# Moving the channel moves and the result stores of a chunked recurrence kernel from SyncE's queue to GpSimd's

## The chip, the cores and the metric

The kernel runs on one core of one Trainium2 chip. The metric is the device time of one execution, in microseconds. Five engines take part: TensorE (PE, with its weight loads shown apart as PEld), VectorE (DVE), ScalarE (ACT), GpSimd (POOL) and SyncE (SP). Each works through its own instructions in order, and semaphores tie them together. A transfer (DMA) is issued by an engine as one of its instructions and then runs by itself.

## The reference

Two parts follow each other: a recurrence over 768 steps for 4 × 8 heads with a 40 × 40 state each, and on its output (4 × 768 × 320) a gated layer with a short convolution in time.

```python
for t in range(S):                      # S = 768; B, H, D = 4, 8, 40
    y[:, :, t] = einsum('bhd,bhde->bhe', r_t, state)
    Sa = einsum('bhde,bhe->bhd', state, a_t)
    state = state * w_t[:, :, None, :] - einsum('bhd,bhe->bhde', Sa, b_t)
    state = state + einsum('bhd,bhe->bhde', v_t, k_t)
x = y.transpose(0, 2, 1, 3).reshape(B, S, H * D)
gate_pre = sum(conv_w[k] * xp[:, k:k + S] for k in range(5))   # xp: x with 4 zero rows ahead
out = (sigmoid(gate_pre) * (x @ w_val)) @ w_out
```

## The kernel before

The 768 steps are cut into 24 chunks of 32. Inside a chunk the recurrence becomes matrix products and a small triangular solve; the state goes from chunk to chunk. All of this stands in `fast_path`. A second path (`general_path`) runs only when a decay lies outside a range; with these inputs it does not run.

Per chunk c, in the names of the plan: `load` brings `ew` (decays, k, b and a; three buffers), `load2` brings `va` and `w` (v in two layouts), `load3` brings `rv` (r, v and r again; one buffer). `rs`, `vs`, `rs1` and `es` (lines 458, 462 and 465) are ScalarE's copies out of `rv`; the next `load3` waits for them. `am`, `u0`, `ut`, `u`, `g`, `ysa`, `ysb` are TensorE's products; `evac_s` makes the next state, `evac_y` (line 532) writes the chunk's output into the tile `xe`, whose rows are heads and positions within a head.

Two chunks make a group for the gated layer; the last two chunks are groups of one, so there are 13 groups. For a group, `xd` moves the outputs from `xe` into the tile `xt`, whose rows are channels: twelve transfers from on-chip memory to on-chip memory, in two halves of eight and four (`x_moves`, line 71). Then come the convolution `cv` (ScalarE line 656, VectorE line 658), the gate (lines 668 to 673), the products `val` (lines 89, 97) and `gv` (line 688), `out` (lines 107, 114), ScalarE's copy `os` (line 703), and `store`, two transfers of 160 KB into the result. Group number gi uses half gi % 2 of the tile `XTW`; its copies `os` go into that same half, which `val` has read by then. So the moves of group gi wait, beside other things, until the stores of group gi − 2 have landed: the list `xw` on line 645 has `("store", pg, 0)` and `("store", pg, 1)`.

What sets the order is `Plan.order`: each step is entered with an engine, an estimated duration in ns and the steps it waits for; a list scheduler runs over these estimates and gives each engine its sequence. TensorE, ScalarE, VectorE and GpSimd carry out exactly that sequence (line 713). SyncE's transfers are not in that list of engines; the framework orders them. In the plan SyncE is nevertheless one engine with durations, so what it is thought to be busy with moves the steps of the others too. Where TensorE would be idle the plan also puts filler products on a constant tile (line 726). The products `val` and `out` of a group are held back until certain later products of the recurrence (`when`, line 679).

Before the change SyncE issues all transfers, and the only line that does it is 317, in the helper `dma`. GpSimd clears three tiles at the start (lines 336, 337, 624) and has nothing to do after that.

Of the kernel before, what the change touches and what calls it, by code (L numbers as in the profile page):

```python
# [16 lines left out]
B, H, S, D = 4, 8, 768, 40  # L17
C = 32
P16 = 16
ER = 104  # L20
DM = 320
# [22 lines left out]
def ac(n):  # L44
    return 154 + 0.833 * n
# [25 lines left out]
def x_moves(xt, xe, L, hf):  # L71

    for h, e0, e1, k, r in (X0, X1)[hf]:
        src = xe[h % 2 * 64 + e0:h % 2 * 64 + e1, h // 2 * 4:h // 2 * 4 + 4, 0:L + 4]
        if k < 2:
            yield xt[r:r + e1 - e0, 4 * k:4 * k + 4, 0:L + 4], src
        else:
            for j in range(2):
                yield xt[j * 64 + r:j * 64 + r + e1 - e0, 8:10, 0:L + 4], src[:, 2 * j:2 * j + 2]
# [20 lines left out]
def out_mms(nc, ps, gv, wo, j, n):  # L100
    T = nc.tensor
    L = n * C
    if n == 2:
        for k in range(3):
            r = slice(j * 64, j * 64 + 64) if k == 2 else slice(0, 128)
            q = 8 if k == 2 else 4 * k + 2 * j
            T.matmul(out=ps, lhsT=gv[r, q * L:q * L + 128], rhs=wo[k][r], start=(k == 0), stop=(k == 2))  # L107
    else:
        for k in range(3):
            for h in range(2):  # L110
                r = slice(h * 64, h * 64 + 64)
                rk = r if k == 2 else slice(0, 128)
                q = 8 * L if k == 2 else (4 * k + 2 * h) * L
                T.matmul(out=ps[r], lhsT=gv[rk, q:q + 64], rhs=wo[k][rk], start=(k == 0), stop=(k == 2))
# [37 lines left out]
class Plan:  # L152
# [6 lines left out]
    def op(self, name, eng, dur, deps, fn, lat=None, give=None):  # L159
        assert name not in self.ops, name  # L160
        self.ops[name] = [eng, dur, list(deps), fn, LAT if lat is None else lat]
        if give:
            self.gives[name] = list(give)
# [100 lines left out]
def fast_path(ctx, tc, ins, out, nch, cst, wts, wz, wmx):  # L264
# [3 lines left out]
    V, A, G, T = nc.vector, nc.scalar, nc.gpsimd, nc.tensor  # L268
# [15 lines left out]
    XTW = const.tile([128, 2 * 680], F32, name="xt")  # L284
# [15 lines left out]
    op = plan.op  # L300

    sg, groups = [], []
    c = 0
    while c < nch:
        n = min(nch - c, 4 if sg else 2)
        sg.append((c, n))
        c += n
    c = 0
    while c < nch:
        n = 2 if c + 2 < nch else 1  # L310
# [5 lines left out]
    def dma(o, i):  # L316
        nc.sync.dma_start(out=o, in_=i)  # L317

    def B2(nm, c):
        return (nm, c, 0), (nm, c, 1)  # L320
# [213 lines left out]
    def slot(nm):  # L534
        return st_["slot", nm]
# [99 lines left out]
    for gi, (c, n) in enumerate(groups):  # L635
        L = n * C
# [4 lines left out]

        def xd(hf, c=c, xt=xt, L=L):
            for o, i in x_moves(xt, st_["xe", c], L, hf):
                dma(o, i)
        xw = [x for j in range(n) for x in B2("evac_y", c + j)] + wl + [("cv", pg, 4, 0), ("cv", pg, 4, 1), ("cv", pg, 4, 2), ("val", pg, 2), ("store", pg, 0), ("store", pg, 1)]
        for hf in range(2):
            op(("xd", c, hf), "SP", (5200, 2600)[hf], xw, lambda hf=hf, xd=xd: xd(hf), 2200)
        xds = [("xd", c, 0), ("xd", c, 1)]
        op(("xd", c), "SP", 1, xds, lambda: None, 2200)
        acc, gv = [AG[:, i * 640:i * 640 + 10 * L].rearrange("p (b t) -> p b t", t=L) for i in range(2)]  # L650
# [43 lines left out]
        for j in range(n):  # L694
            def outm(j=j, c=c, n=n, gf=gf):
                out_mms(nc, slot(("out", c, j))[:, 0:DM], gf, wo, j, n)
            nm = ("out", c, j)
            op(nm, "PE", 1980, prev_gv + om + ([] if late else [when[3 + j]]), outm, give=[("os", c, j)])
            om = [nm]
            prev_out.append(nm)  # L700

            def osc(j=j, c=c, xo=gi % 2 * 680):
                A.copy(out=XTW[:, xo + j * DM:xo + (j + 1) * DM], in_=slot(("out", c, j))[:, 0:DM])
            op(("os", c, j), "ACT", ac(DM), om, osc)

            def store(j=j, c=c, n=n, L=L, xo=gi % 2 * 680):
                dma(out[j * B // n:(j + 1) * B // n, c * C:c * C + L], XTW[:, xo + j * DM:xo + (j + 1) * DM])
            op(("store", c, j), "SP", 800, [("os", c, j)], store, 2200)

    A.preload_act_table_set("natural_log_exp_and_others")  # L710
    E_ = mybir.EngineType
# [1 line left out]
    with tc.manual_schedule(engines={E_.PE, E_.Activation, E_.DVE, E_.Pool}):  # L713
# [3 lines left out]
        for t, e, d, n, fn, s in seq:  # L717
            if s is not None:
                st_["slot", n] = PF[s]
            if e == "PE":  # L720
                lev = min(lev, CAP) - RHO * (t - at)
                at = t
                i = min(range(NS), key=lambda i: free[i])
# [74 lines left out]
def rwkv_kernel(tc, ins, out, nch):  # L798
    with ExitStack() as outer:
        keep = outer.enter_context(tc.tile_pool(name="keep", bufs=1))  # L800
        cst = keep.tile([128, NCST], F32, name="cst")
        wts = keep.tile([128, NWT], F32, name="wts")
        wz = keep.tile([128, 2, DM], F32, name="wz")
        wmx = keep.tile([ER, nch, 2], F32, name="wmx")
        with ExitStack() as ctx:
            fast_path(ctx, tc, ins, out, nch, cst, wts, wz, wmx)
        general_path(tc, ins, out, nch, cst, wts, wz, wmx)
# [69 lines left out]
```

## Time and profile before

| | |
|---|---|
| time, median of 3 runs | 592.12 us (586.3 to 593.3) |
| time of the profiled execution | 591.55 us |
| its span, first to last instruction | 589.5 us |
| busy: PE, DVE, ACT, POOL | 436.1, 408.4, 325.4, 2.5 us |
| mean granted TensorE clock | 0.845 |
| transferred | 58.82 MB, mean 100 GB/s |
| moves `xt<-xe`, stores `out<-xt` | 156 and 24, all issued by SyncE |

The span has three parts: until about 90 us first loads and preparation for several chunks; until about 550 us the chunks one after the other, about 19 us each, with the gated layer of earlier groups between them; then the gated layer of the last groups alone. A row of a group reads: line, engine, operation, output and input tile, count, busy time, mean of one, idle time of the engine just before and what ended it. A row of the waits reads: who waited for whom, total us, times, longest. "SPq" is SyncE issuing a transfer or waiting to.

### The profile page before, as it was taken

The numbers are of one execution on the slowest core, as the hardware profiler recorded it, in microseconds if no ns is written. First come the engines' busy times: TensorE is split into PE (matmuls) and PEld (weight loads), VectorE is DVE, ScalarE is ACT, GpSimd is POOL, SyncE is SP. The second block draws the span as 40 slices with busy tenths as digits, with TensorE's granted clock in tenths as the row PEclk, the third lists the DMA queues.
The fourth block names the chain that finished last, engine by engine and source line by source line (L and its number), as shares of the span: only waits on it lengthen the run. The fifth ranks groups of instructions, "written<-read, shape, count | busy, mean of one in ns | idle before, by whom it ended". The sixth has DMA issues, their size and how long they took to land.

```text
span 589.5 us, 21830 instructions
## 1 busy us (share of the span) xinstructions
PE 436.1 (74%) x9599; PEld 370.1 (63%) x9599; DVE 408.4 (69%) x1025; ACT 325.4 (55%) x652; POOL 2.5 (0%) x8
## 2 busy tenths in 40 slices
PE   4625148983887878889597785879976799789752
PEld 4624137873876767668576675758855677668541
DVE  5379897698887597797485767768965687643230
ACT  4549615554576675787547575764836363554220
POOL 1000000000000000000000000000000000000000
PEclk8857659696999788997797888888997899899866
DMA  8857740242457346445423843514151433311100
GB/s 189 215 135 166 174 121 27 72 97 63 87 131 178 95 112 147 89 126 129 111 53 75 192 101 78 135 53 97 35 138 54 97 92 95 97 43 22 33 19 16
DMA packets 23924, 58.82 MB, mean 100 GB/s; under 512 B 6057, under 2 KB 16553, under 8 KB 21329
## 3 DMA queue, kind: packets, MB, share of 16 engines
q1 hardware_dynamic: 23825, 57.38, 40.3%
q8 instruction: 77, 1.26, 0.9%
q14 instruction: 22, 0.18, 0.1%
HBM read 49.23 MB, written 3.93 MB: 90 GB/s over the span
## 4 chain that ended last, share of the span: by engine, by line
PE 40%; DMA 20%; DVE 17%; ACT 12%; issue 6%; SPq 5%; DVEq 0%; ACTq 0%
DMA rv<-in_rv 6%; PE pc L487 6%; SPq L317 5%; PE pc L508 5%; PE pf L89 4%; DMA ew<-in_ew 4%; DMA out<-xt 4%; PE pf L499 3%; PE pf L411 3%; PE pf L107 3%; DMA w<-in_vw 3%; PE pf L385 3%; PE pc L483 3%; DVE ag L658 3%; PE pc L470 2%
## 5 line engine op out<-in xcount | busy, mean ns | idle before, releaser
L658 DVE SCALAR_TENSOR_TENSOR ag<-xt,wts,ag 128x256 f32<-128x256 f32 (+1 forms) x156 | 60.7, 418 | 32.2 <-ACT ag L656 32.2
L426 DVE TENSOR_TENSOR tm<-x 128x30 f32<-128x30 f32 (+14 forms) x210 | 68.5, 326 | 1.2
L429 DVE TENSOR_TENSOR x<-x,tm 128x30 f32<-128x30 f32 (+14 forms) x210 | 68.4, 326 | 1.1
L458 ACT ACTIVATE rb<-rv,cst 104x512 f32<-104x512 f32 x48 | 34.5, 718 | 48.2 <-DMA rv<-in_rv 48.1
L385 PE MATMUL pf<-kb,qb 104*64 104x64 f32 x768 | 34.6, 258 | 32.6 <-DVE x L429 13.9
L385 PEld LDWEIGHTS pf<-kb,qb 104*64 104x64 f32 x768 | 31.4, 169 | 35.6 <-ACT er L351 18.5
L487 PE MATMUL pc<-ub,T 64*32 64x80 f32 x768 | 39.7, 260 | 12.5 <-issue 9.9
L411 PE MATMUL pf<-cst,kb 104*128 104x104 f32 x192 | 28.6, 290 | 27.3 <-DVE ak L400 18.3
L107 PE MATMUL pf<-wts,ag 128*128 128x320 f32 x132 | 47.5, 483 | 0.0
L726 PE MATMUL pf<-dm 128*128 128x128 f32 x246 | 45.5, 347 | 2.7 <-DVE dm L714 1.1
L351 ACT ACTIVATE er<-ew,bias 104x512 f32<-104x512 f32 x48 | 34.5, 719 | 20.6 <-DVE y L368 12.7
L726 PEld LDWEIGHTS pf<-dm 128*128 128x128 f32 x246 | 40.4, 251 | 5.9 <-issue 2.0
L483 PE MATMUL pc<-T,ub 64*40 64x32 f32 x1536 | 23.4, 215 | 26.9 <-DVE T L441 14.3
L487 PEld LDWEIGHTS pc<-ub,T 64*32 64x32 f32 x768 | 33.2, 123 | 15.9 <-issue 11.7
L89 PE MATMUL pf<-xt,wts 128*128 128x128 f32 (+1 forms) x208 | 37.7, 307 | 7.2 <-DMA xt<-xe 7.2
L346 DVE TENSOR_TENSOR_SCAN lam<-ew,ind 104x528 f32<-104x528 f32 x24 | 30.1, 1255 | 16.4 <-DMA ew<-in_ew 16.4
L499 PE MATMUL pf<-rb,vu 104*64 104x64 f32 x768 | 33.2, 251 | 10.6 <-ACT vu L491 8.0
L502 DVE TENSOR_TENSOR w<-pf,cst 128x512 f32<-128x512 f32 x24 | 16.6, 692 | 34.9 <-PE pf L499 28.0
L411 PEld LDWEIGHTS pf<-cst,kb 104*128 104x128 f32 x192 | 21.1, 158 | 31.1 <-DVE ak L400 18.5
L483 PEld LDWEIGHTS pc<-T,ub 64*40 64x40 f32 x1536 | 20.3, 134 | 32.0 <-ACT ub L478 12.1
L508 PE MATMUL pc<-w,kbt 64*40 64x72 f32 x1536 | 34.1, 236 | 7.8 <-issue 4.4
L499 PEld LDWEIGHTS pf<-rb,vu 104*64 104x64 f32 x768 | 29.5, 162 | 16.2 <-ACT vu L491 11.7
(91 smaller groups left out, 885.2 us busy)
## 6 DMA issues: line engine op xcount, KB each, us to landing
ew<-in_ew SPq DMA_DIRECT2D x24, 838.5 KB
rv<-in_rv SPq DMA_DIRECT2D x24, 624.0 KB
w<-in_vw SPq DMA_DIRECT2D x48, 144.0 KB
va<-in_va SPq DMA_DIRECT2D x24, 160.0 KB
out<-xt SPq DMA_DIRECT2D x24, 160.0 KB
xt<-xe SPq DMA_DIRECT2D x66, 42.5 KB
ag<-in_wts SPq DMA_DIRECT2D x3, 323.0 KB
xt<-in_wts SPq DMA_DIRECT2D x2, 323.0 KB
```

Of the source, the lines that this page charges most:

```text
L89: T.matmul(out=ps[:, j * 2 * L:(j + 1) * 2 * L], lhsT=x[:, m * 128:m * 128 + 128], rhs=xt[:, q:q + 2, 4:4 + L], start=(k == 0), stop=(k == 2))
L107: T.matmul(out=ps, lhsT=gv[r, q * L:q * L + 128], rhs=wo[k][r], start=(k == 0), stop=(k == 2))
L385: T.matmul(out=s[hr(i), j * 64:j * 64 + 64], lhsT=QB[c % NQ][:, pj(j, i)].rearrange("p z t -> p (z t)"), rhs=st_["kb", c][:, pj(j, i)].rea ...
L411: T.transpose(out=s[:, b * 128:b * 128 + ER], in_=src[:, u:u + 2].rearrange("p i f -> p (i f)"), identity=ident[0:ER, 0:ER])
L426: V.tensor_tensor(out=tv, in0=x[:, j:j + 1, j + 1:32].to_broadcast([128, j, n]), in1=x[:, 0:j, j:j + 1].to_broadcast([128, j, n]), op=ALU. ...
L429: V.tensor_tensor(out=x[:, 0:j, j + 1:32], in0=x[:, 0:j, j + 1:32], in1=tv, op=ALU.subtract)
L483: T.matmul(out=PC[hr(z, 40), i, j * C:j * C + C], lhsT=UB[hr(i), j, z], rhs=st_["T", c][hr(i), j], start=True, stop=True)
L487: T.matmul(out=PC[i * 64 + 32:i * 64 + 64, 2 + j // 4, j % 4 * 80:j % 4 * 80 + 80], lhsT=st_["T", c][hr(i), j], rhs=UB[hr(i), j].rearrange ...
L499: T.matmul(out=s[hr(i), j * 64:j * 64 + 64], lhsT=st_["vu", c][:, pj(j, i)].rearrange("p x t -> p (x t)"), rhs=st_["rb", c][:, pj(j, i)].r ...
L508: T.matmul(out=PC[hr(z, 40), j // 4 * 2 + i, j % 4 * 72:j % 4 * 72 + 72], lhsT=l[hr(i, k), j * 2 + z], rhs=rhs[hr(i, k), j * 2 + z], start ...
L658: V.scalar_tensor_tensor(out=acc[:, q], in0=xt[:, q, i:i + L], scalar=cw[:, k, i:i + 1], in1=acc[:, q], op0=ALU.mult, op1=ALU.add)
L726: T.matmul(out=PF[i][:, 0:128], lhsT=dm, rhs=dm, start=True, stop=True)
```

## The change

The twelve moves of a group and its two stores are issued by GpSimd, on its own queue, instead of SyncE. Their plan entries name POOL as engine and carry other estimates: 8000 and 4000 ns for the halves of `xd` instead of 5200 and 2600, 1000 ns for a store instead of 800. What they wait for stays. SyncE keeps the loads of inputs and weights. Arithmetic, tiles and buffers are the same.

```diff
         def xd(hf, c=c, xt=xt, L=L):
             for o, i in x_moves(xt, st_["xe", c], L, hf):
-                dma(o, i)
+                G.dma_start(out=o, in_=i)
...
         for hf in range(2):
-            op(("xd", c, hf), "SP", (5200, 2600)[hf], xw, lambda hf=hf, xd=xd: xd(hf), 2200)
+            op(("xd", c, hf), "POOL", (8000, 4000)[hf], xw, lambda hf=hf, xd=xd: xd(hf), 2200)
...
             def store(j=j, c=c, n=n, L=L, xo=gi % 2 * 680):
-                dma(out[j * B // n:(j + 1) * B // n, c * C:c * C + L], XTW[:, xo + j * DM:xo + (j + 1) * DM])
-            op(("store", c, j), "SP", 800, [("os", c, j)], store, 2200)
+                G.dma_start(out=out[j * B // n:(j + 1) * B // n, c * C:c * C + L], in_=XTW[:, xo + j * DM:xo + (j + 1) * DM])
+            op(("store", c, j), "POOL", 1000, [("os", c, j)], store, 2200)
```

Since the plan's estimates change, the sequences of all engines change, and so does the order of SyncE's transfers. Three places:

SyncE before, between the loads of `rv` for the chunks of steps 448 to 479 and 480 to 511 (from the `va` ahead of the later one; "x2" is two in a row):

```order
L317 DMA va<-in_va 128x320
L317 DMA xt<-xe 40x272 x2
L317 DMA xt<-xe 8x272
L317 DMA xt<-xe 40x272
L317 DMA out<-xt 2x64x320
L317 DMA xt<-xe 8x272
L317 DMA xt<-xe 40x136 x2
L317 DMA xt<-xe 24x136 x2
L317 DMA xt<-xe 40x272 x3
L317 DMA rv<-in_rv 104x1536
```

SyncE now, from the load of `rv` for the earlier to that for the later of these chunks:

```order
L317 DMA rv<-in_rv 104x1536
L317 DMA w<-in_vw 32x1152 x2
L317 DMA va<-in_va 128x320
L317 DMA ew<-in_ew 104x2064
L317 DMA rv<-in_rv 104x1536
```

Twelve moves and a store stood right ahead of the load; now nothing but loads is on this queue.

GpSimd before, from its last memsets to the branch at the end:

```order
L337 MEMSET ub 128x640
L336 MEMSET st 104x1024
L624 MEMSET wz 64x320 x2
L751 TENSOR_LOAD fl
L752 COMPARE_AND_BRANCH
```

GpSimd now, near the end: the stores of the last full group but one, the moves of the group of chunk 22, the stores of the last full group, and the first moves of the group of chunk 23 (`40x4x36` is 40 rows of 4 × 36 values):

```order
L707 DMA out<-xt 2x64x320 x2
L644 DMA xt<-xe 40x4x36 x2
L644 DMA xt<-xe 8x4x36 x2
L644 DMA xt<-xe 40x2x36 x2
L644 DMA xt<-xe 24x2x36 x2
L644 DMA xt<-xe 40x4x36 x4
L707 DMA out<-xt 2x64x320 x2
L644 DMA xt<-xe 40x4x36 x2
```

The moves and stores stand here in whole steps: two stores, twelve moves, two stores. On SyncE one store could stand among the moves.

ScalarE before, at the end of the last chunk (L491 and L495 belong to that chunk, L656 is the first convolution product of the group of chunk 22, L703 copies the results of the last full group, L668 begins the gate of the group of chunk 22):

```order
L491 COPY vu<-pc 104x2x8x32
L495 COPY w<-pc 32x16x40 x2
L656 ACTIVATE ag<-xt,wts 128x128 x2
L656 ACTIVATE ag<-xt,wts 128x64
L703 COPY xt<-pf_115 128x320
L703 COPY xt<-pf_114 128x320
L668 ACTIVATE ag<-ag 128x320
```

ScalarE now, at the same place (L414 copies the flipped state, L673 ends the gate of the last full group):

```order
L414 COPY s_103<-pf_115 128x320
L673 ACTIVATE ag<-ag 128x640
L703 COPY xt<-pf_115 128x320
L703 COPY xt<-pf_116 128x320
L656 ACTIVATE ag<-xt,wts 128x128 x2
L656 ACTIVATE ag<-xt,wts 128x64
L668 ACTIVATE ag<-ag 128x320
```

The two copies that make what the stores of the last full group send stood behind the products that need the moves of the group of chunk 22; now they stand ahead of them.

## The prediction

> **What bounds the kernel now.** I read the page first: busy shares, then the chain of waits by engine.
>
> ```profile
> span 589.5 us, 21830 instructions
> PE 436.1 (74%) x9599; PEld 370.1 (63%) x9599; DVE 408.4 (69%) x1025; ACT 325.4 (55%) x652; POOL 2.5 (0%) x8
> ...
> PE 40%; DMA 20%; DVE 17%; ACT 12%; issue 6%; SPq 5%; DVEq 0%; ACTq 0%
> ```
>
> No engine is full: TensorE is the busiest at 74%, GpSimd is empty. On the chain that ended last a quarter is transfers (DMA 20%) and SyncE's own issuing (SPq 5%). So the second view is what SyncE's queue waited for (total us, times, longest us), and what the engines waited for:
>
> ```profile
> SPq L317 <- DMA out<-xt: 84.4, 18, 7.5
> SPq L317 <- ACT xt L703: 62.7, 12, 15.5
> ```
>
> ```profile
> ACT rb L458 <- DMA rv<-in_rv: 48.1, 12, 7.5
> ...
> ACT ag L656 <- DMA xt<-xe: 22.8, 6, 9.9
> ```
>
> SyncE stands 84.4 us until stores have landed (the moves of a later group overwrite the buffer from which a store reads) and 62.7 us until the copies of L703 have made what a store sends. Everything behind waits too, loads included. ScalarE pays with 48.1 us in twelve waits for `rv`, whose buffer is single. One such place, on SyncE and on ScalarE:
>
> ```profile
> 351.78 0.60 SPq L317 DMA_DIRECT2D out<-xt  x1
> 357.49 6.01 SPq L317 DMA_DIRECT2D xt<-xe  x8
> 363.61 0.44 SPq L317 DMA_DIRECT2D rv<-in_rv  x1
> ```
>
> ```profile
> 352.73 0.62 ACT L465 COPY re<-rv 104x512 f32<-104x512 f32 x1
> ...
> 370.30 0.72 ACT L458 ACTIVATE rb<-rv,cst 104x512 f32<-104x512 f32 x1 [7.10 <-DMA rv<-in_rv]
> ```
>
> L465 is the last reader of the old `rv`; it ends at 353.35. The next load goes out at 363.61, 10.3 us later: SyncE sat until the store of 351.78 had landed, then issued eight moves (6.01 us). ScalarE idles 7.10 us. With nothing ahead of the load it looks like this:
>
> ```profile
> 436.89 0.60 ACT L465 COPY re<-rv 104x512 f32<-104x512 f32 x1
> ...
> 443.97 0.72 ACT L458 ACTIVATE rb<-rv,cst 104x512 f32<-104x512 f32 x1 [4.60 <-DMA rv<-in_rv]
> ```
>
> ```profile
> 437.52 0.32 SPq L317 DMA_DIRECT2D rv<-in_rv  x1
> ```
>
> Issued 0.03 us after its release, it lands 6.4 us later; these 4.60 us are the load itself and stay.
>
> **The change, part by part: what leaves SyncE.** All 156 moves and 24 stores leave; the loads keep their own waits. Pairing each of the twelve `rv` waits with the end of the L465 before it and the issue of the load, four loads went out within 0.1 us and eight had moves or stores ahead; the first and the last of these eight:
>
> ```profile
> 261.83 0.72 ACT L458 ACTIVATE rb<-rv,cst 104x512 f32<-104x512 f32 x1 [1.28 <-DMA rv<-in_rv]
> ...
> 501.71 0.72 ACT L458 ACTIVATE rb<-rv,cst 104x512 f32<-104x512 f32 x1 [3.25 <-DMA rv<-in_rv]
> ```
>
> The lesser of delay and wait, summed over the eight, is 31.6 us of the 48.1: the most that this part can give. It does not all reach the end, since TensorE is late next. Its busy time by stretch (us busy of 50, second figure):
>
> ```profile
> 250.00:300.00 50.00, 40.24 (x976) 34.73 (x978) 36.52 (x92) 32.94 (x66) 0.00 (x0) 0.83 0.43 110
> 300.00:350.00 50.00, 41.01 (x962) 33.81 (x952) 35.03 (x87) 30.87 (x63) 0.00 (x0) 0.88 0.51 120
> 350.00:400.00 50.00, 38.74 (x975) 32.94 (x972) 36.34 (x89) 33.14 (x65) 0.00 (x0) 0.84 0.34 83
> 400.00:450.00 50.00, 42.00 (x962) 35.03 (x961) 39.14 (x105) 26.96 (x55) 0.00 (x0) 0.91 0.36 90
> 450.00:500.00 50.00, 43.45 (x1100) 36.27 (x1096) 37.50 (x101) 26.25 (x51) 0.00 (x0) 0.96 0.33 84
> 500.00:550.00 50.00, 44.51 (x977) 35.54 (x977) 21.84 (x57) 23.58 (x44) 0.00 (x0) 0.97 0.22 53
> ```
>
> The fullest stretch has 44.51 of 50, or 0.89. The four stretches from 250 to 450 hold 162.0 us of TensorE work; at 0.89 they would take 182.0 instead of 200, and 450 to 500 would take 48.8: together 19.2. That lies between nothing and 31.6, and I take **19 us gained**, because a rate that this trace reaches is better evidence than the full sum. The start, until 90 us, keeps its loads and its weights on SyncE in nearly the old order; I cost it at nothing.
>
> **What GpSimd now pays.** Each queue the step passes: SyncE loses 180 issues, GpSimd gets them between its memsets and the end, ordered as written. No trace row shows a transfer issued by GpSimd. The nearest rows (ns, min/median/max) and GpSimd's longest instruction:
>
> ```profile
> L317 SPq DMA_DIRECT2D xt<-xe x156: 637/722/1749, 120.5 to 565.5; - x156
> ```
>
> ```profile
> L336 POOL MEMSET st<- 104x1024 f32 x1 | 1.0, 955 | 0.0
> ```
>
> So an issue costs between 0.64 and 1.75 us; I take 1.1, near the 0.955 us and inside both ends. Twelve moves are then 13.2 us. The planner now counts 12 us for them and has put their readers later; before it counted 7.8. What SyncE needed for twelve is in the rows of the tail:
>
> ```profile
> 540.87 6.87 SPq L317 DMA_DIRECT2D xt<-xe  x8
> 550.26 1.25 SPq L317 DMA_DIRECT2D out<-xt  x2
> 556.28 10.02 SPq L317 DMA_DIRECT2D xt<-xe  x12
> ```
>
> 10.02 against 7.8 planned is 2.2 us late; 13.2 against 12 is 1.2 late. In the middle I therefore cost the slower issue at nothing; the cover is the planner's placing, and it goes when an issue passes about 1.2 us. A group's fourteen transfers at 1.1 us are 15.4 us in two chunks; 24 chunks share what lies between the start (90 us) and the tail (550), 19 us each, so GpSimd itself is no bound. What is queued there behind a waiting store is the next group's moves, which need that store anyway.
>
> In the tail there is no cover. The rows above are in series with these (ScalarE's, TensorE's, then the chain's landings):
>
> ```profile
> 549.14 0.64 ACT L656 ACTIVATE ag<-xt,wts 128x128 f32<-128x128 f32 x2 [9.95 <-DMA xt<-xe]
> ```
>
> ```profile
> 543.37 4.08 PE L107 MATMUL pf<-wts,ag 128*128 128x320 f32 x12
> ```
>
> ```profile
> 565.53 2.02 DMA xt<-xe
> ...
> 578.88 3.87 DMA out<-xt
> ```
>
> The last group's moves wait for the stores of 550.26, and these waited on ScalarE behind L656, which waited for the moves before. GpSimd's price: eight moves at 1.1 instead of 0.86 on average (6.87/8), 1.9 us, and twelve at 1.1 instead of 0.835, 3.2 us. Against that, ScalarE's new order has both L703 copies ahead of L656; their matmuls end at 547.45, so the first can start about then instead of after 549.14+0.64, up to 2.3 us sooner, of which I count 1 (the store still queues behind the moves on GpSimd). Landings I leave at 2.02 and 3.87; the other end is unknown and goes into the range. **Tail: 4 us lost.** The Trainium skill's page "DMA: Bandwidth & Descriptors", section "Latency and other measured facts", gives a first byte after about 1 us for a transfer described by GpSimd's software and 0.6 us for one from SyncE. By that figure four landings in series here would add an estimated 1.6 us; no row of this trace shows it.
>
> **Sum.** 589.5 − 19 + 4 = 574.5 us of span. The profiled execution took 591.55 us, 2.05 more than its span and 0.57 under the median of 592.12, so the time is **576.5 us**, 2.6% below the median.
>
> **The rivals.**
>
> *No change: the loads are early, but little comes of it.* Suppose only the issuing of the moves is saved where it stood on the chain, and loads still land as late, because the moves now run through the same transfer engines beside them. At the place shown that is 6.01 us, and one more place like it as much: 12, less 4 in the tail: 589.5 − 8 + 2 = 583.5; if half of those 12 is given back on TensorE, 589.5. For it speaks that SPq is only 5% of the chain; against it that the waits for landed stores, 84.4 us, are in front of the loads by order alone. This is the outcome that the Trainium skill's page "DMA: Bandwidth & Descriptors", section "Issuing engines are not separate DMA queues", points to: it says transfers from any engine run on the same sixteen DMA engines and that a second issuer saves only the initiating time. By the rule this rival is right; the trace agrees only in part, since 351.78 to 357.49 is a wait and no initiating. Chance 0.25.
>
> *Slower: GpSimd's issue is dear.* Place: the moves of every group and the two last groups. Price at 1.75 us: the tail pays 8 × 0.89 + 12 × 0.915 = 18 instead of 5. In the middle twelve moves take 21 us against 12 planned, 9 late where 2.2 were late before; ScalarE and VectorE work in order, so half of the extra 6.8 us in 11 groups is 37 us. Together −19 + 17 + 37 = +35: 626 us. It decides from about 1.35 us: tail 10, minus 1, middle 0.5 × 11 × 2.0 = 11, sum +1. For it: VectorE is busy 69%, and a move that must wait for one of its instructions would get there. Against: 1.749 is the longest of 156 issues with a median of 0.722, and GpSimd's own longest instruction takes 0.955. The Trainium skill's page "SBUF — State Buffer", section "Who interferes with whom", names such a lock, but only for VectorE's two-port copies and tensor_scalar kinds, not for the two-input forms. Chance 0.19; by the page alone it would be lower, as this kernel's VectorE work in the middle is nearly all two-input.
>
> *More gained.* The new orders use the freed loads fully: −31.6, and moves no dearer than before, 589.5 − 31.6 + 2 = 560. 25.6 of the 31.6 lie between 250 and 450, so TensorE's 162.0 us there would have to fit into 174.4, a rate of 0.93 that no stretch shows. Chance 0.10.
>
> That the change does not do what it says is excluded by the order: SyncE's queue holds loads alone.
>
> **How the numbers follow.** Forecast 0.46, no change 0.25, slower 0.19, more gained 0.10. The first case's own range is 568 to 583 (gain 12 to 26, tail 2 to 6). The whole range is 558 to 604: below, the larger gain; above, an issue of about 1.5 us (tail 13, middle 0.5 × 11 × 3.8 = 21, less the 19 and the 1: +14). 2% of 592.12, about what a measurement of this kernel can tell from no change, sets the bounds at 580.3 and 604.0. Faster: 0.85 of the forecast, all of the larger gain, a little of no change: 0.50. Within 2%: 0.30. Slower: 0.20.
>
> **What would show it.** Right: SyncE's waits for stores and L703 gone; ScalarE's waits for `rv` at 17 to 25 us instead of 48.1; TensorE near 0.88 between 250 and 500; transfers on GpSimd 1.0 to 1.2 us apart; from the last evac_y to the last store's landing some 4 us more. Wrong: moves 1.4 us or more apart with ScalarE's waits for `xt` in mid-kernel well above 22.8 us in all, or `rv` waits that stay because the load itself takes longer.

## The result and the profile after

The changed kernel takes 546.52 us (median of 4 runs, 537.33 to 550.66), the kernel before beside it 589.21 (586.26 to 593.3). The ratio is 0.917, 95% interval 0.902 to 0.933: 8% faster, and 30 us below the forecast of 576.5. Ratios here and below leave out executions that the comparison counts as disturbed, so they differ a little from the quotient of the medians. The kernel before ran beside every experiment too; its medians there lie between 588.9 and 594.5 us.

The profiled execution took 550.66 us, the longest of the four, so the gains read from it are if anything too small. Its page, first the span, the busy shares and the chain that ended last:

```profile
span 548.5 us, 21933 instructions
...
PE 428.9 (78%) x9619; PEld 365.1 (67%) x9619; DVE 407.5 (74%) x1025; ACT 325.8 (59%) x652; POOL 105.0 (19%) x188
...
PE 48%; DVE 17%; DMA 12%; ACT 11%; issue 8%; POOL 1%; SPq 0%; DVEq 0%; POOLq 0%; ACTq 0%
```

Transfers fell from 20% to 12% of the chain and SyncE's issuing from 5% to nothing. GpSimd is busy for 19% of the span and makes 1% of the chain. The waits (total us, times, longest) that answer those shown of before:

```profile
ACT rb L458 <- DMA rv<-in_rv: 9.0, 6, 3.2
...
ACT ag L656 <- DMA xt<-xe: 10.8, 3, 5.7
```

```profile
SPq L317 <- ACT re L465: 191.1, 20, 22.3
...
SPq L317 <- PE pc L470: 51.3, 21, 3.8
```

ScalarE's waits for `rv` went from 48.1 to 9.0 us, those for the moves from 22.8 to 10.8. No load on SyncE (L317) waits behind a landed store or behind L703 any longer; SyncE waits 191.1 us for the reader of the single `rv` buffer, as a queue should that is ahead of its readers.

Where the time went is read best with the first and the last L491 as marks (one per chunk), for both kernels. Columns: us, busy time of PE, PEld, DVE, ACT, POOL with instructions, granted clock, share and rate of transfers. Of before, the middle and the tail:

```profile
94.30:536.70 442.40, 359.70 (x8757) 305.85 (x8757) 323.46 (x811) 267.86 (x524) 0.00 (x0) 0.89 0.40 97
536.70:589.50 52.80, 32.17 (x331) 24.49 (x331) 11.88 (x43) 9.98 (x29) 0.00 (x0) 0.75 0.09 23
```

Of after:

```profile
92.30:493.10 400.80, 342.86 (x8714) 291.09 (x8714) 323.35 (x815) 266.15 (x520) 84.56 (x152) 0.92 0.46 107
493.10:548.50 55.40, 34.57 (x351) 27.26 (x351) 12.69 (x44) 12.30 (x33) 17.99 (x28) 0.75 0.11 24
```

The start gained 2.0 us, the middle 41.6, and the tail lost 2.6: 41.0 in all. In the middle TensorE idled 442.4 − 359.7 = 82.7 us and now idles 57.9: 24.8 of the 41.6. The other 16.8 is TensorE's busy time. It ran 43 fewer products there (8714 against 8757), and 38 of these are fillers. Their rows between the same marks, before and after:

```profile
L726 PE MATMUL pf<-dm 128*128 128x128 f32 x116 | 19.7, 315 | 0.6 <-issue 0.6
```

```profile
L726 PE MATMUL pf<-dm 128*128 128x128 f32 x78 | 12.9, 317 | 0.0
```

That is up to 6.8 us of the 16.8 (the busy times of groups overlap). The remaining 10 us or so is products that took less time each, at a granted clock of 0.92 against 0.89. A filler that is missing does not by itself shorten the kernel (e13 below).

GpSimd's issues (ns, min/median/max, first and last start):

```profile
L644 POOL DMA_DIRECT2D xt<-xe x156: 503/519/696, 111.7 to 522.7; - x156
```

```profile
L707 POOL DMA_DIRECT2D out<-xt x24: 701/828/840, 195.9 to 536.4; - x24
```

A move costs GpSimd 0.52 us where SyncE took 0.72.

### The profile page after: what moved, and what is told of

Read it like the earlier page. It is cut to its first block, busy times and chain, and to the rows that moved or that the text cites. A ratio compares the mean times of both kernels' runs of the same rounds, so it can differ in the third digit from the quotient of the medians.

```text
span 548.5 us, 21933 instructions
## 1 busy us (share of the span) xinstructions
PE 428.9 (78%) x9619; PEld 365.1 (67%) x9619; DVE 407.5 (74%) x1025; ACT 325.8 (59%) x652; POOL 105.0 (19%) x188
## 4 chain that ended last, share of the span: by engine, by line
PE 48%; DVE 17%; DMA 12%; ACT 11%; issue 8%; POOL 1%; SPq 0%; DVEq 0%; POOLq 0%; ACTq 0%
PE pc L508 9%; PE pf L107 7%; PE pc L487 6%; PE pf L89 5%; PE pf L411 4%; PE pc L483 4%; PE pc L474 3%; PE pc L470 3%; ACT w L495 3%; DMA va<-in_va 3%; DMA rv<-in_rv 3%; PE pf L499 3%; PE pf L385 3%; DMA ew<-in_ew 2%; DMA out<-xt 2%
## 5 line engine op out<-in xcount | busy, mean ns | idle before, releaser
L644 POOL DMA_DIRECT2D xt<-xe x156 | 82.9, 538 | 228.8 <-DVE tm L426 115.4
L658 DVE SCALAR_TENSOR_TENSOR ag<-xt,wts,ag 128x256 f32<-128x256 f32 (+1 forms) x156 | 59.2, 413 | 10.8 <-ACT ag L656 10.7
L707 POOL DMA_DIRECT2D out<-xt x24 | 19.6, 818 | 202.6 <-ACT xt L703 196.4
L385 PE MATMUL pf<-kb,qb 104*64 104x64 f32 x768 | 32.4, 247 | 23.1 <-DVE x L429 14.0
L385 PEld LDWEIGHTS pf<-kb,qb 104*64 104x64 f32 x768 | 29.1, 159 | 27.1 <-ACT er L351 18.0
L508 PE MATMUL pc<-w,kbt 64*40 64x72 f32 x1536 | 36.1, 248 | 7.8 <-issue 4.0
L518 DVE TENSOR_TENSOR st<-pc,lam 104x320 f32<-104x320 f32 x46 | 22.2, 486 | 24.3 <-PE pc L508 23.0
L376 ACT ACTIVATE qb<-qa,cst 104x512 f32<-104x512 f32 x48 | 32.5, 714 | 12.6 <-DVE qa L373 11.5
L508 PE MATMUL pc<-re,s 40*40 40x72 f32 x1472 | 33.2, 241 | 7.8 <-ACT w L495 7.5
L508 PEld LDWEIGHTS pc<-w,kbt 64*40 64x40 f32 x1536 | 31.7, 130 | 10.3 <-issue 5.2
```

The source lines that it names most:

```text
L385: T.matmul(out=s[hr(i), j * 64:j * 64 + 64], lhsT=QB[c % NQ][:, pj(j, i)].rearrange("p z t -> p (z t)"), rhs=st_["kb", c][:, pj(j, i)].rea ...
L508: T.matmul(out=PC[hr(z, 40), j // 4 * 2 + i, j % 4 * 72:j % 4 * 72 + 72], lhsT=l[hr(i, k), j * 2 + z], rhs=rhs[hr(i, k), j * 2 + z], start ...
L644: G.dma_start(out=o, in_=i)
L658: V.scalar_tensor_tensor(out=acc[:, q], in0=xt[:, q, i:i + L], scalar=cw[:, k, i:i + 1], in1=acc[:, q], op0=ALU.mult, op1=ALU.add)
```

## The experiments

The first group takes the change apart. It has three parts: which engine issues, which engine the plan counts, and the length of the plan's estimates. "Old" estimates are 5200, 2600 and 800 ns, "new" ones 8000, 4000 and 1000.

**The plan new, the queue old (e1).** TensorE, VectorE and ScalarE have the sequences of the changed kernel; SyncE issues.

```diff
-                G.dma_start(out=o, in_=i)
+                dma(o, i)
...
-                G.dma_start(out=out[...], in_=XTW[...])
+                dma(out[...], XTW[...])
```

> Every engine's sequence is that of the changed kernel, but the moves and stores are issued by SyncE as before. Theory Q (the queue: loads no longer stand behind moves and stores): the gain is gone, ScalarE waits for rv 40 us or more, 585 to 605 us. Theory P (the plan: the new sequences of TensorE, ScalarE and VectorE are better whoever issues): most of the gain stays, 550 to 565 us.

Measured: 592.52 us against 590.79 beside it, ratio 1.017 (1.009 to 1.025): in the range of theory Q, with no gain and at most a small loss. The waits of ScalarE, and of SyncE:

```profile
ACT rb L458 <- DMA rv<-in_rv: 70.0, 12, 12.6
```

```profile
SPq L317 <- DMA out<-xt: 89.1, 19, 8.9
```

The changed kernel's sequences need the early loads: without the new queue the waits for `rv` are 70.0 us, against 9.0 with it and 48.1 in the kernel before. Between this run and the changed kernel only the issuing engine differs, and that is worth 46.0 us.

**The plan old, the queue new (e2).** The sequences of before; GpSimd issues.

```diff
-                dma(o, i)
+                G.dma_start(out=o, in_=i)
...
-                dma(out[...], XTW[...])
+                G.dma_start(out=out[...], in_=XTW[...])
```

> Every engine's sequence is that of the kernel before, but the moves and stores are issued by GpSimd. Theory Q: most of the gain is there, waits for rv under 15 us, 550 to 562 us. Theory P: little of it, 578 to 592 us, with the waits for rv gone and others in their place.

Measured: 579.3 us, ratio 0.977 (0.968 to 0.986).

```profile
ACT rb L458 <- DMA rv<-in_rv: 13.6, 7, 3.3
```

34.5 us of `rv` waits are gone and the median is 11.5 us lower than that of before beside it (590.79). The time lies in the range of theory P, and the waits for `rv` are short, as both theories said. Neither the queue nor the whole new plan alone explains 43 us.

**Moves alone (e3), stores alone (e4).** In plan and queue, with the new estimates for what is moved; the rest as before.

```diff
 e3: xd as in the changed kernel; store and its plan entry as before
 e4: store as in the changed kernel; xd and its plan entries as before
```

> Only the moves go to GpSimd, in plan and queue; stores stay on SyncE. Theory Q with the landings as culprit (84.4 us of SyncE's waits are moves that wait until a store has landed): nearly all of the gain, 548 to 560 us, what is left on SyncE being waits for the copies of L703. If the stores' waits for those copies (62.7 us) hold up loads as much: 565 to 580 us.

> Only the stores go to GpSimd; moves stay on SyncE and still wait there until a store has landed. Theory Q with the landings as culprit: little gain, 575 to 592 us, SyncE's waits for out<-xt stay near 84 us. If the stores' waits for L703 matter most: 555 to 570 us.

Measured: 573.71 us, ratio 0.972 (0.964 to 0.980), and 569.9 us, ratio 0.962 (0.955 to 0.968). Each lies in the range given for the case that the stores' wait for L703 matters. Each rids SyncE of one of its two waits. What is left in e3 and in e4:

```profile
SPq L317 <- ACT xt L703: 101.5, 15, 16.9
```

```profile
SPq L317 <- DMA out<-xt: 92.7, 16, 12.3
```

Moves alone leave the stores' wait for L703, stores alone the moves' wait for landed stores. Taking 24 stores off SyncE is worth no less than taking off 156 moves, which fits that the wait of an issue counts and not its 0.6 or 0.7 us. But each run also carries the longer estimates of what it moves, and e16 below reaches 0.952 with the longer estimates alone, more than e3. So e3 does not show that the moves' new queue gave anything by itself. The product of the two ratios, 0.934, does not reach 0.917.

**The estimates old, all else new (e5).**

```diff
-            op(("xd", c, hf), "POOL", (8000, 4000)[hf], ...)
+            op(("xd", c, hf), "POOL", (5200, 2600)[hf], ...)
...
-            op(("store", c, j), "POOL", 1000, ...)
+            op(("store", c, j), "POOL", 800, ...)
```

> The changed kernel with moves and stores on GpSimd in plan and queue, but with the old estimates: 5200 and 2600 ns for the halves, 800 ns for a store. Theory C (the gain comes from the plan knowing that SyncE's queue is free, together with a queue that is free): the engine named in the plan does it and the size of the estimate does little, so 540 to 556 us, ratio 0.92 to 0.94, and ScalarE's waits for the rv loads stay below 15 us. Rival L (the changed kernel's sequences are one draw among many, and any change of the estimates draws anew): a time anywhere between 547 and 592 us, 570 or more if the draw is a middling one like the two that moved one kind of transfer alone (569.9 and 573.7 us).

Measured: 562.68 us, ratio 0.959 (0.946 to 0.972): above the range of theory C, below that of a middling draw.

```profile
ACT ag L656 <- DMA xt<-xe: 29.3, 11, 8.2
...
ACT rb L458 <- DMA rv<-in_rv: 6.7, 8, 2.0
```

The waits for `rv` are as short as in the changed kernel; those for the moves are 29.3 us instead of 10.8. So the length of the estimates does something by itself.

**The estimates new, all else old (e16); plan on GpSimd with old estimates, queue old (e17); plan on SyncE with new estimates, queue new (e11).** These fill the table.

```diff
 e16, against before:
-            op(("xd", c, hf), "SP", (5200, 2600)[hf], ...)
+            op(("xd", c, hf), "SP", (8000, 4000)[hf], ...)
...
-            op(("store", c, j), "SP", 800, ...)
+            op(("store", c, j), "SP", 1000, ...)
 e17, against before:
-            op(("xd", c, hf), "SP", (5200, 2600)[hf], ...)
+            op(("xd", c, hf), "POOL", (5200, 2600)[hf], ...)
...
-            op(("store", c, j), "SP", 800, ...)
+            op(("store", c, j), "POOL", 800, ...)
 e11, against the changed kernel:
-            op(("xd", c, hf), "POOL", (8000, 4000)[hf], ...)
+            op(("xd", c, hf), "SP", (8000, 4000)[hf], ...)
...
-            op(("store", c, j), "POOL", 1000, ...)
+            op(("store", c, j), "SP", 1000, ...)
```

> GpSimd issues the moves and the stores, as in the changed kernel, and the estimates are the changed kernel's (8000, 4000, 1000), but the plan counts them on SyncE, as before. It is the fourth cell of a table: with GpSimd issuing, SyncE in the plan and old estimates gave 579.3 us, GpSimd in the plan and old estimates 562.7, GpSimd in the plan and new estimates 546.5. Theory M with C (the engine in the plan and the length of the estimate each do their part): L656 waits under 15 us, but loads are planned later than they come, so 555 to 570 us. If the estimate alone does it: 540 to 555 us. Rival (SyncE, counted with 12 us more per group in the plan, is planned full and the steps of the recurrence are put off): 580 us or more.

> The kernel before with the changed kernel's estimates (8000, 4000 and 1000 ns) and nothing else: plan and queue stay SyncE's. TensorE, VectorE and ScalarE have the very sequences that took 558.1 us with GpSimd issuing. Theory H (SyncE's in-order queue holds any sequence near 590 us, since the rv loads stand behind stores and moves): 583 to 596 us, ScalarE's waits for the rv loads 45 us or more. Rival E (the longer estimates were most of it, and would have helped without the new queue): 555 to 575 us.

> The plan counts moves and stores on GpSimd with the old estimates, and SyncE issues them: the sequences that took 562.7 us with GpSimd issuing. Theory H: 583 to 598 us, waits for the rv loads 45 us or more. Rival E does not speak of this one; a time under 575 us would say that the engine named in the plan does the work without the queue, against the 592.5 us of the like run with the new estimates.

Measured: e11 558.09 us (540.49 to 561.94, no interval), in the range of theories M and C together; e16 562.96 us, ratio 0.952 (0.944 to 0.961); e17 606.71 us, ratio 1.023 (1.015 to 1.031). Theory H, that SyncE's queue holds any sequence near 590, falls in e16, where rival E's range holds. In e17 there is no gain either, as H says, but the time is above its range of 583 to 598 us, and the waits for `rv` are 41.4 us where it gave 45 or more; what makes e17 slower than the kernel before was not followed. Changing three numbers of the plan, with not one instruction put on another queue, gives 28.6 us. What SyncE and ScalarE waited for in e16:

```profile
SPq L317 <- DMA out<-xt: 99.8, 19, 9.6
...
SPq L317 <- ACT xt L703: 22.7, 6, 11.2
```

```profile
ACT rb L458 <- DMA rv<-in_rv: 21.5, 7, 7.6
...
ACT ag L656 <- DMA xt<-xe: 15.1, 3, 7.3
```

SyncE still waits for landed stores, but for L703 only 22.7 us instead of 62.7, and ScalarE's two waits fell from 48.1 and 22.8 to 21.5 and 15.1. The whole table, medians in us:

| issues | plan counts | old estimates | new estimates | the estimates' part |
|---|---|---|---|---|
| SyncE | SyncE | before, 588.9 to 594.5 | e16, 562.96 | 28.6 (before beside it: 591.6) |
| SyncE | GpSimd | e17, 606.71 | e1, 592.52 | 14.2 |
| GpSimd | SyncE | e2, 579.3 | e11, 558.09 | 21.2 |
| GpSimd | GpSimd | e5, 562.68 | after, 546.52 | 16.2 |

The longer estimates help in all four rows, by 14 to 29 us. The new queue with a plan that knows of it helps by 29.8 us with the old estimates (e5 against 592.46 beside it; the ratio of 0.959 gives 24) and by 16.4 with the new ones (e16 to after). Each is worth less where the other stands already; both shorten the waits for `rv`, which would explain it (e16 21.5 us, e5 6.7, against 48.1). The waits for the moves are shared less: 15.1 us in e16, but 29.3 in e5, against 22.8. The queue alone, with every sequence but SyncE's and GpSimd's the same, is worth 46.0 us (e1 to after) and 44.0 (e17 to e5) where the plan counts on GpSimd, but 11.5 (before to e2) where it counts on SyncE with the old estimates. The cells come from several chips, so a few us of difference between cells are not read. The weakest cell is e11, whose four executions spread over 21 us; its 4.9 us to e16 are not resolved.

**What a move costs GpSimd (e7, e8).** GpSimd clears an unused tile behind each move, once in e7 and twice in e8; all other sequences are those of the changed kernel.

```diff
+    pad = const.tile([128, 590], F32, name="pad")
...
                 G.dma_start(out=o, in_=i)
+                G.memset(pad, 0.0)
```

> The changed kernel with the same sequences on TensorE, VectorE and ScalarE, but GpSimd clears an unused tile of 128 x 590 behind each of the 156 moves, some 0.58 us, so that a move takes about 1.1 us of its queue: the price that the prediction took, where the trace showed 0.52. The prediction's step (issue time in the middle of the kernel is covered, only the tail pays): two rounds of moves in the tail, the second of which is on the path, so 5 to 10 us more than the changed kernel, 551 to 557 us. Rival (the sequences of the changed kernel live on cheap moves): each of the 13 groups pays a good part of 12 x 0.58 = 7.0 us, 50 to 90 us more, 597 to 637 us.

> The same with the tile cleared twice behind each move: about 1.7 us for a move, near the upper bound 1.75 at which the prediction's slower rival gave 626 us. If issue time is covered in the middle here too: twice the tail of the single clearing, 556 to 570 us. By the slower rival's working, from about 1.35 us on a group's moves come too late for the convolution and each group pays: 600 to 630 us. The waits of ScalarE L656 for the moves, 10.8 us in the changed kernel, tell the two apart: under 40 us, or 80 us and more.

Measured: 564.12 us, ratio 0.959 (0.947 to 0.972), between the two ranges given for e7; and 611.73 us, ratio 1.042 (1.030 to 1.053), in the range that the slower rival's working gave for e8. Groups of instructions in e7 (busy us, mean ns), then e7's wait for the moves and its middle and tail (the added line shifts numbers: L658 is L656 before, L492 is L491):

```profile
L646 POOL MEMSET pad<- 128x590 f32 x156 | 95.4, 612 | 0.0
L645 POOL DMA_DIRECT2D xt<-xe x156 | 83.8, 537 | 195.3 <-DVE tm L427 107.9 <-DVE xe L533 36.7 <-DMA out<-xt 13.2
```

```profile
ACT ag L658 <- DMA xt<-xe: 28.2, 7, 9.8
```

```profile
91.60:502.30 410.70, 350.55 (x8714) 298.94 (x8714) 324.58 (x815) 265.87 (x521) 155.35 (x284) 0.90 0.44 104
502.30:564.20 61.90, 34.72 (x351) 27.27 (x351) 12.79 (x44) 12.37 (x33) 30.67 (x52) 0.75 0.10 22
```

A move then occupies 0.537 + 0.612 = 1.15 us of the queue. The tail grew by 6.5 us, as expected, and the middle by 9.9, which was expected to be covered; the median grew by 17.6. VectorE's busy time in the middle is nearly the same (324.58 us against 323.35), so the clearing did not cost through VectorE. At two clearings (0.535 + 0.610 + 0.591 = 1.74 us) the wait of the same line is

```profile
ACT ag L659 <- DMA xt<-xe: 80.7, 16, 14.9
```

and the kernel is slower than before. By an estimate on a straight line between e7 and e8 it reaches 592 us at about 1.15 + 0.59 × (592 − 564.1)/(611.7 − 564.1) = 1.5 us a move.

**The same price, and the plan told (e12).** e7 with longer estimates.

```diff
-            op(("xd", c, hf), "POOL", (8000, 4000)[hf], ...)
+            op(("xd", c, hf), "POOL", (12700, 6300)[hf], ...)
```

> The changed kernel with GpSimd clearing an unused tile of 128 x 590 behind each move (1.15 us for a move in the trace of that run, 564.1 us), and now the plan is told: 12700 and 6300 ns for the halves, the changed kernel's 8000 and 4000 plus 12 x 0.59. Theory M: the sequences leave the moves the time that they take, L656 waits under 18 us instead of 28.2, and the time falls to 550 to 558 us; what is left over the changed kernel is the tail, 4 to 10 us. If the queue's time itself costs the 17.6 us, whatever the plan knows: 560 us and more.

Measured: 568.17 us, ratio 0.969 (0.959 to 0.980): above the range of theory M (550 to 558), in that of its rival.

```profile
ACT ag L658 <- DMA xt<-xe: 12.3, 2, 9.2
...
ACT rb L459 <- DMA rv<-in_rv: 16.9, 11, 5.6
```

The wait for the moves fell from 28.2 to 12.3 us as theory M said, but the time did not fall with it: other waits came, those for `rv` among them (5.4 in e7). In this run a longer estimate bought the moves time and put something else later.

**How long the estimates should be (e6, e9, e18, e10).** Against the changed kernel's entry for `xd`; what counts for a reader of the moves is the sum of both halves and the landing.

```diff
-  (8000, 4000)[hf], ..., 2200      sum 14.2 us   (changed kernel)
+  (4200, 2100)[hf], ..., 3300      sum  9.6 us   e6, also store 830 and 7400
+  (4200, 2100)[hf], ..., 7900      sum 14.2 us   e9
+  (10000, 5000)[hf], ..., 2200     sum 17.2 us   e18
+  (12000, 6000)[hf], ..., 2200     sum 20.2 us   e10, also store 1500
```

> As the changed kernel, but the plan is given what its trace measured: 4200 and 2100 ns for the halves (twelve moves of 0.52 us), 3300 ns from issue to landing of a move, 830 ns for a store and 7400 ns to its landing, where it had 8000, 4000, 2200, 1000 and 2200. Theory C: truer estimates do no harm, 535 to 550 us, ratio 0.91 to 0.93. Rival L: a new draw, anywhere between 547 and 592 us. If both this and the kernel with the old estimates come out within 2% of the changed kernel (536 to 557 us), the gain is not a lucky draw.

> The changed kernel with the true issue time in the plan (4200 and 2100 ns for the halves, as in the run with measured estimates) but a landing 7900 ns after issue instead of 3300, so that the plan expects a group's moves 14.2 us after it starts them, as in the changed kernel (8000 + 4000 + 2200), and not 9.6 us as in the run with measured estimates or 10.0 us as in that with the old ones. Theory M (an estimate that is longer than the issue keeps ScalarE's L656 from standing in its sequence ahead of the landing): L656 waits under 18 us for the moves (10.8 in the changed kernel, 29.3 and 37.3 in those two) and the time is 540 to 557 us. Rival L (each set of estimates is a draw, and the changed kernel's a lucky one): 560 to 585 us, the level of the other draws.

> The changed kernel with still longer estimates: 12000 and 6000 ns for the halves and 1500 ns for a store, so that the plan expects a group's moves 20.2 us after their start. Theory M: L656 waits no longer than in the changed kernel (under 15 us), and the time is 540 to 560 us, the upper end if the gated layer is put off so far that the tail grows. Rival L: 560 to 585 us.

> The changed kernel with 10000 and 5000 ns for the halves of the moves, 17.2 us in all to their landing where the changed kernel has 14.2 and the run with long estimates 20.2. If the time grows steadily with what is held free beyond the need: 555 to 572 us. If the run with long estimates was a poor draw of the sequences: 542 to 555 us. In both cases the waits of L656 for the moves stay under 16 us.

Measured (no intervals, executions of one kernel up to 22.7 us apart): e6 575.79 us (558.51 to 581.17), e9 555.98 (549.14 to 560.57), e18 556.19 (546.64 to 564.02), e10 581.5 (568.6 to 584.78). ScalarE's waits for the moves, in this order:

```profile
ACT ag L656 <- DMA xt<-xe: 37.3, 11, 9.3
```

```profile
ACT ag L656 <- DMA xt<-xe: 14.2, 6, 7.6
```

```profile
ACT ag L656 <- DMA xt<-xe: 11.1, 4, 5.7
```

```profile
ACT ag L656 <- DMA xt<-xe: 11.7, 3, 6.0
```

With moves and stores on GpSimd in plan and queue, the wait follows the sum: 37.3 us at 9.6, 29.3 at 10.0 (e5), 10.8 to 14.2 from 14.2 on. Between e6 and e9 the time falls too, 575.8 to 556.0, but their lowest executions are only 9.4 us apart (558.51 and 549.14), and e6 also counts 7400 ns for the landing of a store, so the two do not differ by the moves alone. Estimates that are true to the issue time (e6: 4200 and 2100 for 6.2 us measured) are worse than the changed kernel's of twice that. Beyond 14.2 the wait stays: at 17.2 (e18) the time is that of e9, on the border between what a slope and what a poor draw of the sequences would give; at 20.2 (e10) it is 581.5 us, in the range of rival L and not explained by these waits. So part of the differences among these kernels may be sequences that happen to suit; e9 has the changed kernel's sum and is 9.5 us slower, so the changed kernel lies at the good end of them.

**TensorE's clock (e13, e14, e15).** The plan adds filler products on TensorE; these runs change their number and leave all other sequences alone.

```diff
 e13, against the changed kernel:
+                k = min(k, 0) if t > 90000 else k
                 for _ in range(k):
 e14, against the changed kernel; e15, against before:
-RHO, CAP, DUM = 0.37, 700, 250
+RHO, CAP, DUM = 0.55, 700, 250
```

> The changed kernel without the plan's filler products on TensorE behind 90 us of its plan (75 instead of 133 of them), all other steps in the same sequences. Theory K (TensorE's clock is granted the more, the less it stands idle): the granted clock between 90 and 500 us falls from 0.92 to 0.86 to 0.89, and at the 3.4 us of a hundredth that the executions of single kernels show the time is 556 to 568 us. Rival N (fillers don't matter for the clock, they only take TensorE's time): clock 0.91 to 0.93, time 538 to 548 us.

> The changed kernel with more filler products (235 instead of 133; the activity that the plan keeps up is 0.55 instead of 0.37). Theory K: the clock between 90 and 500 us is 0.92 to 0.95, time 536 to 548 us, no gain if the waits and not the clock are left. Rival N: clock unchanged, 102 more products of 0.55 to 1.1 us, of which those that delay a step are lost, 550 to 570 us.

> The kernel before with more filler products (223 instead of 123), moves and stores on SyncE as they were. Theory K: the clock between 90 and 500 us rises from 0.88 to 0.90 to 0.93, and the time falls by 7 to 17 us against the kernel before, ratio 0.97 to 0.99, since the waits for rv stay. Rival N: clock 0.87 to 0.89, ratio 1.00 to 1.03.

Measured: e13 546.8 us, ratio 0.924 (0.916 to 0.933); e14 564.61, ratio 0.948 (0.937 to 0.959); e15 592.21, ratio 0.997 (0.991 to 1.003). Between 90 and 500 us of the changed kernel, of e13 and of e14:

```profile
90.00:500.00 410.00, 350.16 (x8852) 297.66 (x8853) 327.59 (x826) 270.55 (x527) 87.97 (x158) 0.92 0.45 105
```

```profile
90.00:500.00 410.00, 345.34 (x8878) 292.93 (x8874) 328.08 (x827) 271.00 (x530) 91.72 (x164) 0.90 0.45 105
```

```profile
90.00:500.00 410.00, 352.67 (x8634) 302.86 (x8631) 320.16 (x806) 262.43 (x514) 82.56 (x150) 0.90 0.45 104
```

In this stretch the clock does not follow the fillers: 0.90 with fewer and with more of them, 0.92 in the changed kernel. Over the whole span it does: 0.84 to 0.86 in the four executions of e13, 0.86 to 0.87 in those of the changed kernel, 0.87 to 0.89 in e14's; and 0.84 to 0.87 in e15 against 0.79 to 0.84 in before beside it. But the time does not: fewer fillers cost nothing, more of them cost 18 us in the changed kernel and nothing in the one before. Theory K's times failed in all three. Among executions of one kernel time often falls with the clock (e6: 581.17 us at 0.823, 558.51 at 0.870), but not always: of the kernel before beside it one took 586.07 us at 0.820 and one 604.8 at 0.828. That the clock makes the time is not shown.

## Why the prediction was wrong, point by point

*The direction and the mechanism* were right: SyncE's in-order queue held the loads, and freeing it is worth time. The waits of SyncE's loads for stores and L703 went, as foreseen; ScalarE's waits for `rv` fell to 9.0 us, below the 17 to 25 foreseen. Of the 48.1 us the forecast had let at least 16.5 stay (48.1 − 31.6), as the load's own time; in the new sequences even that is mostly covered.

*The step that failed is the gain, "19 us gained".* The middle gained 41.6 us and the start 2.0, where 19 and nothing were forecast. It was mis-sized in two ways.

First, it took TensorE's 162.0 us between 250 and 450 as fixed and let only idle time go, up to the rate 0.89. The rate itself was a fair guess. Over the middle it went from 359.7/442.4 = 0.813 to 342.86/400.8 = 0.855, and the five stretches of after that answer those shown of before hold 217.6 us of 250, or 0.87, where 0.88 was foreseen:

```profile
250.00:300.00 50.00, 40.98 (x977) 35.34 (x977) 40.62 (x96) 34.92 (x71) 14.04 (x26) 0.90 0.59 141
300.00:350.00 50.00, 43.08 (x1084) 35.90 (x1081) 42.81 (x106) 38.26 (x78) 7.81 (x14) 0.97 0.54 123
350.00:400.00 50.00, 45.83 (x1274) 38.71 (x1273) 44.22 (x109) 38.51 (x76) 15.67 (x28) 1.00 0.49 108
400.00:450.00 50.00, 45.11 (x1165) 37.47 (x1163) 46.11 (x131) 32.20 (x61) 13.28 (x24) 1.00 0.39 92
450.00:500.00 50.00, 42.63 (x1126) 34.55 (x1127) 26.40 (x68) 25.68 (x48) 15.27 (x27) 0.97 0.29 70
```

At the middle's new rate the old 359.7 us would have taken 420.5, a gain of 21.9, close to the 19. The other 19.7 us (16.8/0.855) are products that became shorter and fillers that left the middle (up to 6.8 of the 16.8): the stretches from 350 to 450 hold 1274 and 1165 products where before had 975 and 962, at a granted clock of 1.00 where it had 0.84 and 0.91. The trace of before had shown the clock moving between 0.83 and 0.97 from stretch to stretch; the forecast read past it. Why it rose, and whether the higher clock shortened the kernel, stays open (e13 to e15).

Second, it read the plan's new numbers only as a cover for a slower issue ("In the middle I therefore cost the slower issue at nothing"). e16 shows that these numbers alone, on the old queue, give 28.6 us: more than was forecast for the whole change. Both of ScalarE's waits fell there, and SyncE's for L703. Of these the forecast counted the `rv` waits alone, and only as far as the queue is the cause; the 22.8 us of L656 it quoted and left as they were, asking only whether the new engine's issue would be covered. That a later place in the plan shortens the waits for the moves is shown by the estimates of different length (29.3 us in e5, 10.8 in the changed kernel); through which steps it frees SyncE from L703 in e16 was not followed.

*The price of a move* was bounded by 0.64 to 1.75 us and taken at 1.1; it is 0.52, below the lower bound. The nearest rows, an issue by another engine and a memset, did not bound it. e7 puts a move at 1.15 us and so tests the sum at its own price: 564.1 us against 576.5. Of the miss of 30 us, 17.6 are thus the price and 12.4 the gain net of the rest. In e7 the middle pays 9.9 us, so "nothing" for the middle was wrong at that price; in the changed kernel the question did not arise.

*The tail* was put at 4 us lost and lost 2.6, for other reasons. GpSimd's issues, and when the last copies and landings came:

```profile
508.21 1.63 POOL L707 DMA_DIRECT2D out<-xt  x2 [4.12 <-ACT xt L703]
514.85 1.90 POOL L644 DMA_DIRECT2D xt<-xe  x3 [5.02 <-DVE ag L688]
517.71 5.62 POOL L644 DMA_DIRECT2D xt<-xe  x9 [0.96 <-DMA out<-xt]
```

```profile
508.21 8.81 DMA out<-xt x2
...
536.38 4.60 DMA out<-xt
```

The row of the two stores in the same place before:

```profile
550.26 5.88 DMA out<-xt
```

Twelve moves take 7.5 us of issue instead of 10.02, so no price was paid there. But the two stores issued at 508.21 have landed only at 517.02, and the nine moves of 517.71 wait for that: 8.81 us against 5.88. The last landing is 4.60 us against 3.87. The stores' landings were the part that cost; the forecast had left landings "at 2.02 and 3.87". The Trainium skill's page "DMA: Bandwidth & Descriptors", section "Latency and other measured facts", had pointed there with an estimated 1.6 us over four landings. These two rows of stores agree in sign and are 3.7 us longer together; the landing of the last moves, 1.36 us against 2.02, goes the other way:

```profile
522.68 1.36 DMA xt<-xe
```

*The rivals.* The slower one was right that late moves cost the middle, and its condition was false: at 1.74 us a move e8 takes 611.7 us where it gave 626, with the waits at L656 at 80.7, and it decides from about 1.5 us, by the estimate above, rather than 1.35. The larger gain (560 us) was thought to need a rate of 0.93 "that no stretch shows"; the kernel passed it with less TensorE time in the middle. The no-change rival, 583.5 to 589.5 us, comes near in time to what the queue alone does where the plan is the old one, 579.3 in e2. Its condition, that loads still land as late, does not hold there: the waits for `rv` fell from 48.1 to 13.6 us. So in time only, and only in e2, do the runs come near the rule that this rival came from (the same page of the Trainium skill, "Issuing engines are not separate DMA queues"). Where the plan counts on GpSimd, the queue alone is worth 46.0 and 44.0 us (e1 to after, e17 to e5). In the first of these pairs ScalarE's waits for `rv` fell from 70.0 to 9.0 us, so what stood behind SyncE's waiting issues is a large part of what was saved.

## What to carry to other kernels

Where a scheduler lays out in-order engines, a change of a queue is two changes, the queue and the layout, and so are the estimates that come with it: try the estimates alone before crediting the queue. Here an estimate that covered the time until the data can be read, with room (14.2 us in all for moves issued in 6.2), did better than one near the issue time, and 20.2 us did worse; the best length was not looked for any closer than that. And a cap drawn from TensorE's busy time must leave its products' length free to change when the granted clock in the rows is below 1.

## What the runs showed of the hardware

GpSimd issues an on-chip move in 0.52 us and a 160 KB store in 0.83 (SyncE: 0.72 and 0.60; medians). With VectorE busy for 74% of the span the longest of the 156 moves took 0.70 us. Issued by GpSimd, moves land after 3.3 us and stores after 7.4 (medians; min, median, max of each):

```profile
DMA to landing us min/median/max: 1.6/3.3/7.7
```

```profile
DMA to landing us min/median/max: 4.6/7.4/11.6
```

The single landings that the prediction quoted of SyncE's were 2.02 and 3.87 us, and the pair of stores above took 5.88; no row gives SyncE's median. The median store on this queue thus lands later than any price that was in the sum, and the plan of the changed kernel, which counts 2200 ns for it, does not know.
